# When twenty tiles are picked for routing, and where two weight pieces are decoded: one core's program for attention and experts

## The chip, the cores and the metric

One Trainium2 chip, one core of it. The metric is device time in microseconds (us) of one execution. Before the change the median of three runs is 911.4 us (911.33 to 913.87).

## The reference

Three stages follow each other. Attention with a decaying state gives 3072 rows of 384 numbers (4 batches of 768 steps, 8 heads of 48). A router then gives each row to one of 8 experts, 384 rows each, greedily by the largest score over all pairs of a row and an expert. Each expert is a two-layer network with a rectifier. Last comes a gated network that all rows share.

```python
for t in range(S):
    cur = np.einsum('bhd,bhe->bhde', u[None] * kt, vt)
    y[:, :, t] = np.einsum('bhd,bhde->bhe', rt, state + cur)
    state = w[None, :, :, None] * state + np.einsum('bhd,bhe->bhde', kt, vt)
...
flat = (x @ w_gate).flatten()
for idx in np.argsort(-flat):
    tok, e = (int(idx) // E, int(idx) % E)
    if assigned[tok] >= 0 or counts[e] >= cap:
        continue
    assigned[tok] = e
    counts[e] += 1
...
out[mask] = np.maximum(x[mask] @ w1[e], 0.0) @ w2[e]
...
return (a * b @ w_out)      # a = x @ w_a, b = x @ w_b
```

## The kernel before, in words

The program is written for five in-order engines and no scheduler reorders it: what stands earlier in the Python text of an engine's work is issued earlier on that engine.

**Attention** is a loop over 24 tiles of 128 rows, j = 0 to 23 (L715). An iteration works on several tiles at once. SP issues the loads of tile j+3 (`load_na`, `load_rk`) and j+2 (`load_va`). POOL makes q and K of tile j+3 (`prep_a`, L558, L559, L599). DVE makes `kh` and `rh` of tile j+2 (L611, L615) and sums q of that tile (`cc`, L607); ACT spreads `cc` on diagonals (L620). PE makes the scores of tile j+1 into the one buffer `pair` (L627), and DVE copies them under a mask (L631): since `pair` is single, the scores of the next tile wait for this copy. Then PE makes the rows and router scores of tile j-1 (`rows`, L676), DVE sums those into `LG` (L680), and PE makes the output of tile j (`y_out`, L662 and L666). From j = 20 on the state is no longer updated.

**Decoding.** The weights of the last network come as 64-bit numbers. A piece of 128x384 is fetched by SP (L85) and decoded by one ACT pass (L92), four DVE instructions (L95, L97, L99, L101), and a copy on ACT with a subtraction on POOL (L103, L104). 24 pieces belong to `w_a` and `w_b`, 12 to `w_out`. `EARLY` (L41) is how many of the 24 are decoded in attention, one an iteration: piece k is fetched at j = k, its ACT pass stands in j = k+1, the rest in j = k+2 (`side`, L716). In attention the DVE instructions work in a PSUM bank, later in SBUF. The other pieces and `w_out` are decoded by the generator `late` (L999). It is advanced once after every few matmuls of the expert stage (`step`, L901); a piece takes as many steps as its inner loop has rounds.

**Routing.** The greedy assignment is found by eight searches. The first needs `pick` (L159: ten small DVE instructions that find each row's best expert and its key) and `compare` (L199: the keys against 128 limits, four tiles to an instruction unit), for all 24 tiles; `head` (L214) does both for a range of tiles. Twenty tiles are done inside the loop, four after it, and PE counts the flags (`count`, L209). What `pick` and `compare` read (`un`, `steps`, and more) is set by POOL in iteration 20 (L756 to L769). The later searches (`route`, `settle`) run on DVE beside the experts' matmuls, as generators advanced by the same `step`.

**Experts.** For each of eight experts: weights gathered by POOL, split in two parts by ACT and POOL (L804, L805), matmuls L893 and L933, with ACT, DVE and POOL between them (L937, L938, L966, L969, L971, L972).

Of the kernel before, what the change touches and what calls it, by code (L numbers as in the profile page):

```python
# [37 lines left out]
DELAY = 0.8  # L38
LATE = 0, 1, 3, 5, 7
PACE = 0.8, 0.9, 0.8, 1.2  # L40
FIRST, EARLY = 2, 21  # L41
LEAST, MOST = (float(np.int32(x).view(np.float32)) for x in (0x38000000, 0x47EFFFFF))


def tile_kernel(tc, rkt, nat, wt, ub, wg, ca, cf, w12, wa, wb, wo, out):
    nc = tc.nc
    v, act, pool, pe = nc.vector, nc.scalar, nc.gpsimd, nc.tensor
    with ExitStack() as ctx:
# [23 lines left out]
        def small():  # L72
            return shared[:, 0:128]
# [9 lines left out]
        def fetch64(src, space, bufs):  # L83
            raw = space.tile([128, 768], I32, name="raw64", bufs=bufs)
            nc.sync.dma_start(raw, src.bitcast(I32))  # L85
            return raw

        def decode64(dst, raw, space, bufs):
# [18 lines left out]
        wab_pieces = [(WAB[i][:, d, q], (wa, wb)[i][d * 128:(d + 1) * 128, q * 384:(q + 1) * 384])  # L107
                      for q in range(4) for i in range(2) for d in range(3)]
# [50 lines left out]
        def pick(ml, s, kd):  # L159
            m, ki, top, q, i = [x[:, s] for x in best[:5]]  # L160
            ohu = best[5][:, :, s].rearrange("p e t -> p t e")
            n = s.stop - s.start
            b = m.bitcast(I32)

            def e(a):
                return a[:, :, None].to_broadcast([128, n, NE])

            rv = revb[:, None, :].to_broadcast([128, n, NE])
            v.tensor_reduce(m, ml[:, s], axis=AX, op=OP.max)
            yield 0.5  # L170
            v.tensor_tensor(q, ml[:, s], e(m), op=OP.is_equal)
            v.tensor_scalar(ki, b, 31, 0x7fffffff, op0=OP.arith_shift_right, op1=OP.bitwise_and)
            yield 0.5
            v.tensor_tensor(q, q, rv, op=OP.mult)
            v.tensor_tensor(ki, b, ki, op=OP.bitwise_xor)
            v.tensor_reduce(i, q, axis=AX, op=OP.max)
            yield 0.5
            if kd is not None:
                v.tensor_scalar(top, ki, 25, None, op0=OP.arith_shift_right)
            v.tensor_tensor(q, rv, e(i), op=OP.is_equal)  # L180
            if kd is not None:
                v.tensor_scalar(kd[:, s], top, 64.0, None, op0=OP.add)
            v.tensor_tensor(ohu, q, e(un[:, s]), op=OP.mult)  # L183
            yield 0.5
# [11 lines left out]
        def flags(T):  # L196
            return [wide([384 // T, T, 4]) for _ in range(T // 64)]

        def compare(ge, T, kd, s):  # L199
            n = 1536 // T  # L200
            while s.start < s.stop:
                g, end = s.start // n, min(s.stop, s.start // n * n + n)
                a, b = (s.start - g * n) // 4, (end - g * n) // 4
                v.tensor_tensor(ge[g][:, a:b], steps[:, None, 0:T].to_broadcast([128, b - a, T, 4]),
                                kd[:, s.start:end].rearrange("p (a c) -> p a c", c=4)[:, :, None]
                                .to_broadcast([128, b - a, T, 4]), op=OP.is_le)
                s = slice(end, s.stop)
# [6 lines left out]
        def head(parts):  # L214
            T = ROUNDS[0][0]
            if parts[0].start == 0:
                K["ge"] = flags(T)
                K["kd"] = R.tile([128, NT], BF, name="kd", bufs=2)
                K["cnt"] = small()[0:T, 0:NE]
            s = slice(parts[0].start, parts[-1].stop)  # L220
            for _ in pick(LG, s, K["kd"]):
                pass
            for x in parts:
                compare(K["ge"], T, K["kd"], x)
# [280 lines left out]
        with ExitStack() as actx:  # L505
# [95 lines left out]
            def prep_a(j):  # L601
                prep_q(j)
                prep_k(j)

            def prep_cc(j):
                CC[j] = A.tile([128, NH], F32, name="cc", bufs=2)
                v.tensor_reduce(CC[j], Q[j], axis=AX, op=OP.add)  # L607
# [14 lines left out]
            def scores(j):  # L622
                ps = pair.rearrange("p (g a t) -> p g a t", g=2, a=4)
                for i in range(4):
                    for g in range(2):
                        o = slice(g * 64, g * 64 + HD)
                        pe.matmul(ps[:, g, i], KH[j][o, i], RH[j][o, i], start=True, stop=True)  # L627
                return ps

            def masked(j, ps):  # L630
                v.copy_predicated(AT[j].rearrange("p g a t -> p (g a) t"), mask[:, None, :].to_broadcast([128, 8, 128]),  # L631
                                  ps.rearrange("p g a t -> p (g a) t"))
# [82 lines left out]
            for j in range(NT):  # L715
                def side(n):  # L716
                    if 0 <= j + n - FIRST < EARLY:
                        next(decode[j + n - FIRST])

                for n, load in ((3, load_na), (3, load_rk), (2, load_va)):  # L720
                    if j + n < NT:
                        load(j + n)
                if 0 <= j + 2 - FIRST < EARLY:
                    raws.append(fetch64(wab_pieces[j + 2 - FIRST][1], A, 3))
                if j + 3 < NT:
                    prep_a(j + 3)
                if 0 <= j + 1 - FIRST < EARLY:
                    decode.append(decode64(wab_pieces[j + 1 - FIRST][0], raws[j + 1 - FIRST], A, 3))
                side(1)
                for make in (prep_kh, prep_rh):  # L730
                    if j + 2 < NT:
                        make(j + 2)
                    side(0)
                if j == 0:
                    masked(1, scores(1))
                if j + 2 < NT:
                    prep_cc(j + 2)
                side(0)
                side(0)
                if 1 <= j < NT - 1:  # L740
                    masked(j + 1, scores(j + 1))
                    rows(j - 1)
                y_out(j)
                state(j)
                if j == NT - 1:
                    rows(j - 1)
                if j + 2 < NT:
                    prep_c(j + 2)
                state_out(j)
                side(0)  # L750
                if j == 2:
                    v.tensor_copy(rw[:, 0:8], cfs[:, 0:8])
                    v.tensor_copy(rw[:, 8:16], cfs[:, 136:144])
                    v.tensor_copy(unrev, rev)
                    v.tensor_copy(cbs, cbf)
                if j == 20:  # L756
                    for x, value in [(un, 1.0), (Aoh, 0.0), (cB, float(CAP)), (cE, float(CAP))]:
                        pool.memset(x, value)
                    pool.memset(runs, 1.0)
                    pool.memset(runs.rearrange("p (e t) -> p e t", e=NE)[:, :, 0], 0.0)  # L760
                    for k in range(NK):
                        pool.memset(groups[:, k], 128 * k)
                    for x, t in scaled.items():
                        pool.memset(t, x)
                    for k in range(4):
                        pool.memset(field.rearrange("p (h k) -> p h k", h=2)[:, :, k], 32.0 ** k)
                        pool.memset(fmask[:, k:k + 1], 31 << 5 * k)
                    pool.tensor_copy(steps, cfs[:, 8:136, None].to_broadcast([128, 128, 4]))
                    pool.tensor_copy(iota4, cbf[:, 128:256, None].to_broadcast([128, 128, 4]))  # L769
                if j == 22:  # L770
                    head([slice(0, 8), slice(8, 16), slice(16, 20)])
            rows(NT - 1)
            count(K["cnt"], K["ge"], ROUNDS[0][0], slice(0, 20))
            warm(IDLE[2], accum)
# [223 lines left out]

        def late():  # L999
            todo = [(WO[:, f], wo[f * 128:(f + 1) * 128]) for f in range(NFF)]  # L1000
            todo[9:9] = wab_pieces[EARLY:]
            raw = [fetch64(x[1], M, 2) for x in todo[:2]]
            parts = [decode64(x[0], raw.pop(0), M, 2) for x in todo[:1]]
            next(parts[0])
            for i in range(len(todo)):
                if i + 2 < len(todo):
                    raw.append(fetch64(todo[i + 2][1], M, 2))
                for n in range(9):
                    yield
                    if n == 4 and i + 1 < len(todo):  # L1010
                        parts.append(decode64(todo[i + 1][0], raw.pop(0), M, 2))
                        next(parts[1])
                    elif n in LATE:
                        next(parts[0])
                parts.pop(0)
# [95 lines left out]
```

## Time and profile before

| | |
|---|---|
| median of the runs | 911.4 us |
| the profiled execution's own time | 919.04 us |
| its span | 917.3 us |
| busy, share of the span: PE, DVE, POOL, ACT | 92%, 68%, 50%, 37% |
| attention, to the last rows of tile 23 | 0 to 146.6 us of the span |
| first search, without experts beside it | 146.6 to 180 us |
| first expert, with the second search beside it | 180 to 290 us |

The profiled execution is 7.6 us longer than the median. Times of the trace are counted from the start of its span. A row of the timeline has start, duration, engine, line, operation, output and inputs; what stands in square brackets is the idle time of that engine just before, and what ended it. Instructions of an engine overlap by some tenths of a microsecond, so the distance between two starts is a better price than a duration.

### The profile page before, as it was taken

Reading aid. Unit: us, or ns where it says so; the run is one execution under the profiler, and the core shown is the slowest. Engines: PE = TensorE matmul, PEld = TensorE weight load, DVE = VectorE, ACT = ScalarE, POOL = GpSimd, SP = SyncE. Lnnn points to the kernel's source line nnn. Section 1 sums busy time; section 2 is a strip of 40 time slices with the busy share of each in tenths; the row PEclk is TensorE's granted clock in tenths of the full one; section 3 lists DMA queues with packets and bytes.
Section 4 is the critical chain, followed back from the end, with each engine's and each line's share of the span. In section 5 each row is a group of like instructions: output and inputs, shape, how many; then the busy total and the mean of one; then the engine's idle time right before and its main releaser. Section 6 shows DMA issues by size and latency. Waiting matters only on the chain.

```text
span 917.3 us, 16061 instructions
## 1 busy us (share of the span) xinstructions
PE 845.0 (92%) x6109; PEld 811.0 (88%) x6109; DVE 627.1 (68%) x1694; ACT 341.1 (37%) x804; POOL 456.5 (50%) x509
## 2 busy tenths in 40 slices
PE   6788789789987999999999999999999899999994
PEld 6777778778977998999899989998999899999994
DVE  6899988598899878878777687778777612112111
ACT  4798972233233322332323233223322233323221
POOL 7688861442456515644463555265525654614221
PEclk7899989888998999999999999999999999999998
DMA  8889961421240203202020302030203212200000
GB/s 284 295 300 322 322 237 63 137 79 52 79 138 18 78 1 95 69 28 69 27 79 18 87 10 95 1 96 23 73 1 96 62 59 69 70 1 27 1 1 26
DMA packets 28142, 82.24 MB, mean 90 GB/s; under 512 B 4128, under 2 KB 10912, under 8 KB 28064
## 3 DMA queue, kind: packets, MB, share of 16 engines
q1 hardware_dynamic: 19872, 46.59, 14.9%
q0 software_dynamic: 8192, 34.61, 12.2%
q8 instruction: 48, 0.79, 0.3%
q14 instruction: 30, 0.25, 0.1%
HBM read 71.75 MB, written 9.44 MB: 89 GB/s over the span
## 4 chain that ended last, share of the span: by engine, by line
PE 69%; DVE 21%; DMA 3%; issue 3%; ACT 2%; SPq 1%; another core or an unknown queue 0%; POOL 0%; POOLq 0%; ACTq 0%; DVEq 0%
PE ab L893 26%; PE acc L893 24%; PE ab L933 10%; DMA rk<-in_rkt_dram 3%; DVE at L631 2%; PE pair L627 1%; PE acc L148 1%; PE acc L676 1%; PE acc L666 1%; DVE cB L491 1%; DVE sg L969 1%; DVE xt L826 1%; DVE ohu L183 1%; PE acc L662 1%; DVE mk L488 1%
## 5 line engine op out<-in xcount | busy, mean ns | idle before, releaser
L972 POOL TENSOR_TENSOR hg<-sg,hg 128x384 fp32r<-128x384 f32 x95 | 99.1, 1044 | 267.6 <-ACT hg L971 262.1
L893 PE MATMUL ab<-ym,Wb 128*128 128x384 f32 x864 | 173.5, 341 | 6.2 <-DVE sg L969 6.1
L893 PE MATMUL acc<-WO,hg 128*128 128x384 f32 x864 | 175.0, 344 | 0.0
L893 PE MATMUL ab<-ym,Wa 128*128 128x384 f32 x864 | 173.6, 342 | 0.0
L893 PEld LDWEIGHTS ab<-ym,Wb 128*128 128x128 f32 x864 | 150.6, 189 | 10.5 <-DVE sg L969 10.2
L893 PEld LDWEIGHTS acc<-WO,hg 128*128 128x128 f32 x864 | 153.9, 191 | 3.9 <-ACT sg L966 3.3
L893 PEld LDWEIGHTS ab<-ym,Wa 128*128 128x128 f32 x864 | 152.2, 191 | 1.8 <-issue 0.5
L805 POOL TENSOR_TENSOR wr<-raw,wr 128x384 fp32r<-128x384 f32 x120 | 121.3, 1035 | 55.9 <-ACT wr L804 55.5
L969 DVE TENSOR_TENSOR sg<-ab,sg 128x384 f32<-128x384 f32 (+1 forms) x98 | 53.4, 546 | 118.4 <-PE ab L893 105.4
L971 ACT ACTIVATE hg<-sg 128x384 fp32r<-128x384 f32 (+1 forms) x98 | 50.8, 520 | 198.7 <-DVE sg L969 194.1
L933 PE MATMUL ab<-xt,wr 128*128 128x384 f32 x567 | 114.0, 345 | 0.0
L893 PE MATMUL acc<-hg,wr 128*128 128x384 f32 x576 | 110.1, 338 | 0.9 <-DVE hg L938 0.9
L933 PEld LDWEIGHTS ab<-xt,wr 128*128 128x128 f32 x567 | 102.4, 195 | 0.0
L893 PEld LDWEIGHTS acc<-hg,wr 128*128 128x128 f32 x576 | 100.8, 189 | 1.3 <-DVE hg L938 1.2
L797 POOL DMA_INDIRECT raw<-in_w_dram,widx x64 | 64.3, 1005 | 54.0 <-issue 22.5
L966 ACT ACTIVATE sg<-ab 128x384 f32<-128x384 f32 x96 | 46.8, 488 | 106.9 <-PE ab L893 102.9
L804 ACT ACTIVATE wr<-raw 128x384 fp32r<-128x384 f32 x128 | 59.8, 515 | 48.4 <-PE acc L893 22.7
L938 DVE SCALAR_TENSOR_TENSOR hg<-ab,hg 128x384 fp32r<-128x384 f32 x64 | 35.5, 555 | 53.7 <-ACT hg L937 53.6
L937 ACT ACTIVATE hg<-ab 128x384 fp32r<-128x384 f32 x64 | 31.5, 492 | 87.0 <-PE ab L933 79.6
L620 ACT ACTIVATE at<-ident,cc 128x128 f32<-128x128 f32 x192 | 58.6, 394 | 3.2 <-DVE cc L607 3.2
L627 PE MATMUL pair<-rh,kh 48*128 48x128 f32 x384 | 31.4, 309 | 27.4 <-DVE at L631 24.8
L627 PEld LDWEIGHTS pair<-rh,kh 48*128 48x128 f32 x384 | 26.5, 210 | 30.6 <-DVE at L631 27.6
(213 smaller groups left out, 1211.7 us busy)
## 6 DMA issues: line engine op xcount, KB each, us to landing
rk<-in_rkt_dram SPq DMA_DIRECT2D x24, 512.0 KB, 5.5
na<-in_nat_dram SPq DMA_DIRECT2D x24, 384.0 KB, 4.7
va<-in_nat_dram SPq DMA_DIRECT2D x24, 200.0 KB, 5.6
raw<-in_wa_dram SPq DMA_DIRECT2D x12, 384.0 KB, 6.0
xrows<-xr SPq DMA_DIRECT2D x24, 192.0 KB, 3.4
raw<-in_wb_dram SPq DMA_DIRECT2D x12, 384.0 KB, 5.8
raw<-in_wo_dram SPq DMA_DIRECT2D x12, 384.0 KB, 3.0
raw<-in_w_dram,widx POOLq DMA_INDIRECT x64
```

The lines of the kernel that those rows point to most:

```text
L620: act.activation(AT[j][:, h % 2, h // 2], ident, AF.Copy, scale=CC[j][:, h:h + 1])
L627: pe.matmul(ps[:, g, i], KH[j][o, i], RH[j][o, i], start=True, stop=True)
L797: pool.indirect_dma_start(out=RAW[p, f], out_offset=None, in_=w12f, in_offset=bass.IndirectOffsetOnAxis(ap=WIDX[p][:, f:f + 1], axis=0))
L804: act.activation(t[:, 0], raw, AF.Copy)
L805: eng.tensor_tensor(t[:, 1], raw, t[:, 0].bitcast(F32), op=OP.subtract)
L893: pe.matmul(dst, lhs(a), rhs(b), start=first and i == 0, stop=last and i == 2)
L933: pe.matmul(ph, WR[p, f, 0][:, a, d * 128:(d + 1) * 128], XT[p][:, b, d], start=i == 0, stop=i == 8)
L938: v.scalar_tensor_tensor(t[:, 1], ph, 0.0, t[:, 0].bitcast(F32), op0=OP.max, op1=OP.subtract)
L966: act.activation(sg, pab[0], AF.Copy)
L969: v.tensor_tensor(sg[:, c], pab[1][:, c], sg[:, c], op=OP.mult)
L971: act.activation(t[:, 0, c], sg[:, c], AF.Copy)
L972: (v if end else pool).tensor_tensor(t[:, 1, c], sg[:, c], t[:, 0, c].bitcast(F32), op=OP.subtract)
```

## The change

Twenty tiles are picked in two steps: tiles 0 to 15 at the end of iteration 20, tiles 16 to 19 at the end of iteration 22, where all twenty were before. POOL's setting of what these need moves from iteration 20 to iterations 14, 15, 16 and 18. `EARLY` falls from 21 to 19: pieces 19 and 20 are no longer fetched and decoded in iterations 19 to 22 but by `late`, which now has 17 pieces instead of 15, takes 8 steps for each instead of 9, and begins the five pieces of `w_a` and `w_b` after seven of `w_out` instead of nine.

```diff
-FIRST, EARLY = 2, 21
+FIRST, EARLY = 2, 19
...
-                if j == 20:
+                if j == 14:
                     for x, value in [(un, 1.0), (Aoh, 0.0), (cB, float(CAP)), (cE, float(CAP))]:
                         pool.memset(x, value)
                     pool.memset(runs, 1.0)
                     pool.memset(runs.rearrange("p (e t) -> p e t", e=NE)[:, :, 0], 0.0)
+                if j == 15:
                     for k in range(NK):
                         pool.memset(groups[:, k], 128 * k)
...
+                if j == 16:
                     pool.tensor_copy(steps, cfs[:, 8:136, None].to_broadcast([128, 128, 4]))
+                if j == 18:
                     pool.tensor_copy(iota4, cbf[:, 128:256, None].to_broadcast([128, 128, 4]))
+                if j == 20:
+                    head([slice(0, 8), slice(8, 16)])
                 if j == 22:
-                    head([slice(0, 8), slice(8, 16), slice(16, 20)])
+                    head([slice(16, 20)])
...
-            todo[9:9] = wab_pieces[EARLY:]
+            todo[7:7] = wab_pieces[EARLY:]
...
-                for n in range(9):
+                for n in range(8):
```

**DVE from the router scores of tile 19 to the masked copy of tile 22** (L680 `LG`; L611, L615, L607 prepare tile 23; L95 to L101 decode piece 19; L631 is the masked copy). Before:

```order
L680 TENSOR_REDUCE LG<-acc_69 128x8
L611 TENSOR_TENSOR kh<-rk,table_106 128x512
L95 TENSOR_SCALAR acc_70<-mag 128x384
L615 TENSOR_TENSOR rh<-rk,table_105 128x512
L97 TENSOR_SCALAR acc_70<-acc_70 128x384
L607 TENSOR_REDUCE cc<-q 128x8
L99 SCALAR_TENSOR_TENSOR acc_70<-raw_1767,acc_70 128x384
L101 SCALAR_TENSOR_TENSOR mag<-raw_1767,acc_70 128x384
L631 COPY_PREDICATED at<-mask,pair 128x1024
```

Now, from the second half of the pick of tiles 0 to 15 on:

```order
L176 TENSOR_REDUCE i<-q 128x16
L179 TENSOR_SCALAR top<-ki 128x16
L180 TENSOR_TENSOR q<-cbs,i 128x128
L182 TENSOR_SCALAR kd<-top 128x16
L183 TENSOR_TENSOR ohu<-q,un 128x16x8
L204 TENSOR_TENSOR wide<-steps,kd 128x1024
L204 TENSOR_TENSOR wide<-steps,kd 128x512 x2
L611 TENSOR_TENSOR kh<-rk,table_106 128x512
L615 TENSOR_TENSOR rh<-rk,table_105 128x512
L607 TENSOR_REDUCE cc<-q 128x8
L631 COPY_PREDICATED at<-mask,pair 128x1024
```

The four decode instructions are gone, and ten instructions of the pick and three of the compare (L169 to L204) stand ahead of `kh`.

**POOL at the same place** (q and K of tile 23, then the subtraction of a decoded piece). Before:

```order
L559 TENSOR_TENSOR q<-q,na 128x384
L599 TENSOR_TENSOR KT_144<-na,kn 128x384
L104 TENSOR_TENSOR Wa<-mag,Wa 128x384
L758 MEMSET un 128x24
L758 MEMSET Aoh 128x192
```

Now:

```order
L559 TENSOR_TENSOR q<-q,na 128x384
L599 TENSOR_TENSOR KT_144<-na,kn 128x384
L104 TENSOR_TENSOR Wa<-mag,Wa 128x384
L802 DMA raw<-in_w_dram,widx 128x768 x2
L817 DMA row<-xrows,idx 128x384 x3
```

The three tensor instructions stay; what followed them in the loop has moved up to iterations 14 to 18 or left attention.

**DVE in the second search, in the first expert** (L204 are the compares for which PE waits; L95 to L101 are the decoding by `late`). Before:

```order
L183 TENSOR_TENSOR ohu<-q,un 128x24x8
L204 TENSOR_TENSOR wide<-steps,kd 128x512 x2
L938 SCALAR_TENSOR_TENSOR hg<-ab_2438,hg 128x384
L95 TENSOR_SCALAR mag<-mag 128x384
L204 TENSOR_TENSOR wide<-steps,kd 128x512
L97 TENSOR_SCALAR mag<-mag 128x384
L204 TENSOR_TENSOR wide<-steps,kd 128x512
L99 SCALAR_TENSOR_TENSOR mag<-raw_2711,mag 128x384
L204 TENSOR_TENSOR wide<-steps,kd 128x512 x2
```

Now:

```order
L183 TENSOR_TENSOR ohu<-q,un 128x24x8
L95 TENSOR_SCALAR mag<-mag 128x384
L97 TENSOR_SCALAR mag<-mag 128x384
L204 TENSOR_TENSOR wide<-steps,kd 128x512 x2
L943 SCALAR_TENSOR_TENSOR hg<-ab_2428,hg 128x384
L99 SCALAR_TENSOR_TENSOR mag<-raw_2698,mag 128x384
L204 TENSOR_TENSOR wide<-steps,kd 128x512 x2
L101 SCALAR_TENSOR_TENSOR mag<-raw_2698,mag 128x384
L204 TENSOR_TENSOR wide<-steps,kd 128x512 x2
```

The decode instructions come sooner: two stand ahead of the first compares where none did, and four ahead of the last where three did.

## Rows read from the trace of the kernel before

**Rows 1.** Page: the chain that ended last, shares of the span by engine.
```profile
PE 69%; DVE 21%; DMA 3%; issue 3%; ACT 2%; SPq 1%; another core or an unknown queue 0%; POOL 0%; POOLq 0%; ACTq 0%; DVEq 0%
```
**Rows 2.** Chain in order of time (start, us, what): two loads of attention.
```profile
101.97 7.79 DMA rk<-in_rkt_dram
...
127.75 5.63 DMA rk<-in_rkt_dram
```
**Rows 3.** Timeline, DVE, iterations 20 to 23 and the last pick.
```profile
132.59 0.18 DVE L680 TENSOR_REDUCE LG<-acc 128x8 f32<-128x32 f32 x1
133.40 0.69 DVE L611 TENSOR_TENSOR kh<-rk,table 128x512 f32<-128x512 f32 x1 [0.63 <-DMA rk<-in_rkt_dram]
...
137.05 1.29 DVE L631 COPY_PREDICATED at<-mask,pair 128x1024 f32<-128x1024 int32 x1
138.33 0.54 DVE L95 TENSOR_SCALAR acc<-mag 128x384 f32<-128x384 f32 x1
...
140.58 1.31 DVE L631 COPY_PREDICATED at<-mask,pair 128x1024 f32<-128x1024 int32 x1
141.87 0.31 DVE L169 TENSOR_REDUCE m<-LG 128x20 f32<-128x160 f32 x1
...
144.13 2.29 DVE L204 TENSOR_TENSOR wide<-steps,kd 128x1024 bf16<-128x1024 bf16 x4
...
146.87 0.19 DVE L169 TENSOR_REDUCE m<-LG 128x4 f32<-128x32 f32 x1
...
148.09 0.45 DVE L204 TENSOR_TENSOR wide<-steps,kd 128x512 bf16<-128x512 bf16 x1
```
**Rows 4.** Timeline, PE: scores after a long wait, and at the end of attention.
```profile
114.78 2.08 PE L627 MATMUL pair<-rh,kh 48*128 48x128 f32 x16 [2.42 <-DVE at L631]
...
121.71 0.53 PE L640 MATMUL shared<-va,KT 128*48 128x48 f32 x16
...
135.83 1.08 PE L666 MATMUL acc<-at,va 128*48 128x128 f32 x16
138.39 1.16 PE L627 MATMUL pair<-rh,kh 48*128 48x128 f32 x16 [1.48 <-DVE at L631]
...
142.48 1.16 PE L662 MATMUL acc<-rh,SD 128*128 128x128 f32 x8
```
**Rows 5.** Timeline, POOL: one subtraction in iteration 14, then iteration 20.
```profile
95.13 1.01 POOL L104 TENSOR_TENSOR Wb<-mag,Wb 128x384 fp32r<-128x384 f32 x1 [0.63 <-ACT Wb L103]
...
132.98 1.00 POOL L559 TENSOR_TENSOR q<-q,na 128x384 f32<-128x384 f32 x1
133.94 1.01 POOL L599 TENSOR_TENSOR KT<-na,kn 128x384 f32<-128x384 f32 x1
135.19 1.01 POOL L104 TENSOR_TENSOR Wa<-mag,Wa 128x384 fp32r<-128x384 f32 x1 [0.24 <-ACT Wa L103]
```
**Rows 6.** Line L180 of the pick: ns min/median/max of nine, and one beside POOL.
```profile
L180 DVE TENSOR_TENSOR q<-cbs,i x9: 193/353/897, 143.2 to 710.7; 128x192 bf16<-128x192 bf16 x7, 128x160 bf16<-128x160 bf16 x1, 128x32 bf16<-128x32 bf16 x1
...
710.39 1.02 POOL L972 TENSOR_TENSOR hg<-sg,hg 128x384 fp32r<-128x384 f32 x1 [3.72 <-ACT hg L971]
...
710.73 0.89 DVE L180 TENSOR_TENSOR q<-cbs,i 128x192 bf16<-128x192 bf16 x1
```
**Rows 7.** PE's longest wait, 180 to 291 us: us in total, times, longest.
```profile
PE shared L212 <- DVE wide L204: 4.9, 5, 2.4
```
**Rows 8.** Stretches: busy PE, PEld, DVE, ACT, POOL; clock, DMA share, GB/s.
```profile
185.00:209.00 24.00, 18.23 (x116) 17.00 (x116) 23.62 (x54) 8.37 (x19) 11.34 (x11) 0.86 0.19 61
...
265.00:290.00 25.00, 19.87 (x106) 18.74 (x105) 24.41 (x64) 7.35 (x18) 13.48 (x13) 0.93 0.13 44
```
**Rows 9.** DVE groups by line, 185 to 290 us: busy us, mean ns.
```profile
L99 DVE SCALAR_TENSOR_TENSOR mag<-raw,mag 128x384 int32<-128x384 int32 x14 | 11.4, 811 | 0.2
L101 DVE SCALAR_TENSOR_TENSOR mag<-raw,mag 128x384 int32<-128x384 int32 x14 | 8.4, 602 | 0.2
L95 DVE TENSOR_SCALAR mag<-mag 128x384 f32<-128x384 f32 x14 | 7.2, 516 | 0.0
L97 DVE TENSOR_SCALAR mag<-mag 128x384 int32<-128x384 int32 x14 | 6.8, 486 | 0.3
```

## The prediction

> **What bounds the kernel now.** I read first the chain that ended last: PE holds 69% of the span and DVE 21% [rows 1], so a microsecond of PE is a microsecond of time, and DVE counts where PE waits for it. The change touches two such places. The one is the end of attention, read in the timelines of DVE, PE and POOL from iteration 20 on; the reader is to see there which DVE instruction lets PE begin its last unbroken run. The other is the first expert, read in the list of PE's waits and in busy time by stretch: PE waited 4.9 us for the compares of the second search [rows 7], in a stretch in which DVE was busy for 23.62 of 24 us [rows 8].
>
> At the end of attention DVE finished the scores of tile 19 at 132.77, stood 0.63 us for the load of tile 23, and began `kh` at 133.40; the masked copy of tile 22 began at 137.05 [rows 3]. PE had stood for 1.48 us and went on at 138.39 with the scores of tile 23 [rows 4]. From there PE did the scores, one set of rows, both outputs and the last rows with no gap: attention ends as late as that masked copy ends plus a fixed run of PE. The pick of twenty tiles lay beside this run: it began at 141.87, and its compares took 2.29 us from 144.13 on [rows 3], beside PE's second output, which began at 142.48 [rows 4]. It cost little where it stood. So the price of the new order is: when does the masked copy of tile 22 begin?
>
> **The change, part by part, at the end of attention.** The path from `kh` to that copy was 137.05 - 133.40 = 3.65 us and held three preparations and four decode instructions. The same four alone, one iteration later, took 140.58 - 138.33 = 2.25 us [rows 3]. So without piece 19 the path is 1.4 us by difference; three times the 0.69 of `kh` would be 2.1. I take 1.6, nearer to the difference, as starts overlap.
>
> Ahead of it now stand the pick and the compare of sixteen tiles. A pick took 144.13 - 141.87 = 2.26 us for twenty tiles and 148.09 - 146.87 = 1.22 for four, so 2.0 for sixteen; the compare took 2.29 for twenty and 0.45 for four, so 1.8 [rows 3]. Together 3.8 us. If nothing disturbs them they run from 132.77 to 136.6, the load lands inside that, and the masked copy begins at 136.6 + 1.6 = 138.2, against 137.05: **1.1 us late**. That is the lower end.
>
> But they will be disturbed. POOL makes q and K of tile 23 and a subtraction just then: 132.98 to 133.98, 133.94 to 134.95, 135.19 to 136.20 [rows 5]. An instruction of the pick that met a POOL multiply of 1.02 us took 0.89 us, ending where the multiply ended plus its usual length; its median is 0.353 [rows 6]. Attention's other DVE work passed POOL undisturbed, so this meeting is new here. If one locked instruction is held by each of the three, the last gets through at 136.2, and about 0.5 us of pick and 1.8 of compare remain: 138.5, and the copy begins at 140.1, **3.0 us late**. I take this one, since POOL is busy for three of the 3.4 us that the pick needs to start clear. The rows show the holding for this one instruction plainly; where the others of its kind may pass, the value falls towards 1.1.
>
> The Trainium skill (SBUF — State Buffer, "Who interferes with whom") goes further than these rows: a VectorE instruction with two SBUF inputs, and one in a two-port mode, blocks against a GpSimd instruction that reads SBUF, while a reduction never does. By it the second, third and fourth instruction of the pick would each meet a POOL instruction, 1.4 us of pick would be left at 136.2, and the copy would be 4.0 us late instead of 3.0. No row of this case shows the second or fourth one held.
>
> **PE's clock.** Before the scores of tile 23 PE would stand 1.48 + 3.0 = 4.5 us. After a wait of 2.42 us the same scores took 2.08 us instead of 1.16, and the four groups from the scores to the output took 121.71 - 114.78 = 6.93 us against 142.48 - 138.39 = 4.09 after the wait of 1.48 [rows 4]: the matmuls ran at the lower level, half of the full clock, and **2.8 us** were lost. I take that loss in full, since PE's run from there to the end of attention has no gap to absorb it. If the wait stays at 1.1 + 1.48 = 2.6 us it is still above 2.42, but so close that it may go either way; there I take nothing, and the loss is in the range.
>
> What leaves costs nothing more and gains nothing more: ACT's and POOL's passes for the two pieces and two fetches of 384 KB on SP's queue were beside PE's waits for DVE; the 0.63 us for the load is covered by the pick. SP's later stores of rows only move up. POOL's settings in iterations 14 to 18 are a few tenths each; POOL stood 0.63 us in such an iteration before its subtraction [rows 5], and q and K are made an iteration ahead of their use, so a delay is caught up. If that cover were gone, what an iteration's settings take beyond 0.63 us would be added to it, in four iterations at most. The second pick of four tiles (1.22 + 0.45 us) falls in DVE's wait for the last rows.
>
> **In the first expert.** Two pieces more are decoded there. On DVE one costs 0.516 + 0.486 + 0.811 + 0.602 = 2.4 us as a mean with the holding by POOL in it [rows 9], two cost 4.8: the upper end. The lower end is 0, if all of it falls where PE runs on. It does not: with 8 steps instead of 9 the instructions come sooner, and by the order printed for the second search one more of them stands ahead of the last compare that PE waits for. By the same order one more stands in the next chain from the search's result to the one-hot tables, and two more in the stretch from 265 to 290 us, where DVE was busy for 24.41 of 25 us and PE for 19.87 [rows 8]. Four instructions at 0.5, the price of the two short ones, which come sooner most often, make **2.0 us**. The other four find gaps where PE is full. ACT (8.37 of 24 us) and POOL (11.34 of 24) have room for the two passes each adds, and the DMA share of 0.19 leaves room for the fetches [rows 8]. The pieces are not late: the first of them is used at step 117 by the loops, and all five are done by step 96 where three were by step 108.
>
> **Sum.** 3.0 + 2.8 + 2.0 = 7.8 us slower. Against the profiled execution's 919.04 that is 926.8; that execution is 7.6 us above the median of the runs shown, and the metric is the median, so 911.4 + 7.8 = 919.2. The bounds: 1.1 + 0 + 0 = +1.1, and 4.0 + 2.8 + 4.8 = +11.6.
>
> **The rivals.** *POOL holds, the clock stays.* The masked copy is 3 us late but the matmuls keep full clock, as after the wait of 1.48 us. 3.0 + 2.0 = +5.0: 916.4. Against it: the wait would be three times that one.
>
> *POOL does not matter.* The pick slips between POOL's instructions, +1.1, and one microsecond of decoding shows: +2.1, or 913.5, which a measurement cannot tell from no change. For it: three starts of POOL leave small gaps, and only one instruction of the pick is seen held in my rows.
>
> *The load of the last tile is late, and the pick fills a hole: faster.* The place is `kh` of tile 23. In the trace its load took 5.63 us in the chain and cost 0.63 us of DVE, but another one held the chain for 7.79 us [rows 2], and the plain runs are 7.6 us shorter than the profiled one, so their waits need not lie where the trace has them. If in them the load lands after the end of the pick, from about 137 to 138.5, 3.5 to 5 us later than traced, the pick is free, the path from the load is 1.6 instead of 3.65, and with two fetches of 384 KB gone from beside it the load itself may come sooner, by an estimated 1 us of its 5.63. PE's wait would have been 5 us before and a drop of the clock with it, which may go: -2.05 - 1 - 2.8 + 2.0 = -3.9, so 907.5. Against it: by this point the loads are nearly over, and DVE waited only once.
>
> **How the numbers follow.** About 0.3% or 2.7 us is what a measurement of this kernel can tell from no change: 908.7 to 914.1. The forecast has 0.42, the full clock with POOL's holding 0.20, the undisturbed pick 0.18, the late load 0.17; 0.03 is for a search delayed by the whole 4.8 us. That gives faster 0.18, same 0.17, slower 0.65. The likeliest is 919.2. The range goes from 908.5, which takes in half of the late-load case, to 922.5, near the sum of the upper ends; less than 2 in 10 is left out.
>
> **What would show it.** Right: in the changed profile the first pick has L172, L180 or L183 longer than alone, beside POOL's L559, L599 or L104; the masked copy of tile 22 begins 3 us later counted from the scores of tile 19; PE stands over 4 us before the scores of tile 23, and these take some 2.1 us; PE's waits in the first expert grow by 2 us. Wrong: those scores begin no later than before, or take 1.16 us; `kh` of tile 23 waits for its load after the pick; PE's waits for DVE in the first expert are no longer than now.

## The result, and the profile after

After the change the kernel takes 921.34 us (median of 12 runs, 917.65 to 926.4), before it 912.11 us (12 runs of the same comparison). These two medians lie 9.2 us apart. The ratio of the comparison, which I use throughout, is 1.0081, with a 95% interval from 1.0063 to 1.01: slower by 7.4 us, between 5.7 and 9.1. The forecast was 7.8 us more, 919.2 us, in a range from 908.5 to 922.5.

The profiled execution after took 920.48 us with a span of 918.7, only 1.4 us more than that of before. The two aren't comparable as a whole: in the profile of before, loads earlier in attention were late and the router scores of tile 19 came at 132.59 us, in that of after at 126.33, and the run with two pieces decoded twice (below), whose attention is that of before, had them at 126.65. So I compare by stretches: (1) from the router scores of tile 19 to the start of the last rows (L676 for tile 23, a group of 16 matmuls), and (2) from there to the end of the span.

The page of after, the chain that ended last, shares by engine, against [rows 1]:

```profile
PE 66%; DVE 27%; issue 3%; DMA 1%; ACT 1%; POOL 1%; SPq 0%; POOLq 0%; DVEq 0%; ACTq 0%
```

DVE stands in the chain with 27% where it had 21%. The timeline of DVE of after, from the scores of tile 19 to the masked copy of tile 23, against [rows 3] (start, duration, and in brackets the wait before):

```profile
126.33 0.17 DVE L680 TENSOR_REDUCE LG<-acc 128x8 f32<-128x32 f32 x1
126.42 0.26 DVE L169 TENSOR_REDUCE m<-LG 128x16 f32<-128x128 f32 x1
126.72 0.95 DVE L171 TENSOR_TENSOR q<-LG,m 128x128 bf16<-128x128 f32 x1
127.59 0.97 DVE L172 TENSOR_SCALAR ki<-m 128x16 int32<-128x16 int32 x1
...
128.93 0.17 DVE L179 TENSOR_SCALAR top<-ki 128x16 int32<-128x16 int32 x1
129.04 1.07 DVE L180 TENSOR_TENSOR q<-cbs,i 128x128 bf16<-128x128 bf16 x1
...
130.50 1.57 DVE L204 TENSOR_TENSOR wide<-steps,kd 128x1024 bf16<-128x1024 bf16 x3
131.98 0.68 DVE L611 TENSOR_TENSOR kh<-rk,table 128x512 f32<-128x512 f32 x1
...
133.64 1.28 DVE L631 COPY_PREDICATED at<-mask,pair 128x1024 f32<-128x1024 int32 x1
...
137.16 1.29 DVE L631 COPY_PREDICATED at<-mask,pair 128x1024 f32<-128x1024 int32 x1 [2.18 <-PE pair L627]
```

POOL of after at the same time, against [rows 5]:

```profile
126.52 1.00 POOL L559 TENSOR_TENSOR q<-q,na 128x384 f32<-128x384 f32 x1
127.48 1.06 POOL L599 TENSOR_TENSOR KT<-na,kn 128x384 f32<-128x384 f32 x1
128.97 1.00 POOL L104 TENSOR_TENSOR Wa<-mag,Wa 128x384 fp32r<-128x384 f32 x1 [0.43 <-ACT Wa L103]
```

Three instructions of the pick are long, and each ends where one of POOL's three has ended: L171 at 127.67 behind L559 (127.52), L172 at 128.56 behind L599 (128.54), L180 at 130.11 behind L104 (129.97). The copy of tile 22 begins 133.64 - 126.33 = 7.31 us after the scores of tile 19; before it was 137.05 - 132.59 = 4.46 [rows 3]. It is 2.85 us late.

PE of after, from the end of the output of tile 21 to the last rows, against [rows 4]:

```profile
129.56 1.08 PE L666 MATMUL acc<-at,va 128*48 128x128 f32 x16
134.97 2.08 PE L627 MATMUL pair<-rh,kh 48*128 48x128 f32 x16 [4.33 <-DVE at L631]
136.97 2.03 PE L676 MATMUL acc<-iw,yt 128*128 128x104 f32 x8
138.80 1.44 PE L662 MATMUL acc<-rh,SD 128*128 128x128 f32 x8
140.18 1.08 PE L666 MATMUL acc<-at,va 128*48 128x128 f32 x16
...
143.28 2.03 PE L676 MATMUL acc<-iw,yt 128*128 128x104 f32 x16
```

PE stands for 4.33 us where it stood for 1.48, and its next 16 matmuls take 2.08 us instead of 1.16; the granted clock was 0.50 of full speed from 135 to 139 us. Stretch 1 takes 143.28 - 126.33 = 16.95 us, against 11.99 before (the last rows began there at 144.58): **+4.96**.

The three longest of PE's waits of after, 180 to 291 us, against [rows 7] (us in total, times, longest):

```profile
PE ab L898 <- DVE sg L974: 4.3, 2, 2.2
PE shared L212 <- DVE wide L204: 4.0, 3, 2.5
PE ab L480 <- DVE sums L476: 3.6, 1, 3.6
```

And the two stretches of [rows 8] in after (busy PE, PEld, DVE, ACT, POOL; clock, DMA share, GB/s); the experts begin 1.3 us earlier here, so the work in them is not quite the same:

```profile
185.00:209.00 24.00, 18.48 (x102) 17.36 (x102) 23.38 (x61) 7.75 (x17) 8.50 (x8) 0.76 0.17 50
265.00:290.00 25.00, 17.80 (x93) 16.33 (x92) 24.45 (x66) 8.68 (x20) 12.03 (x12) 0.93 0.13 40
```

Stretch 2 takes 918.7 - 143.28 = 775.42 us, against 917.3 - 144.58 = 772.72: **+2.70**. The compares, in which I saw the cost, account for less than before (4.0 against 4.9); the time went elsewhere in the first experts, where DVE is as full as it was.

### The profile page after: what moved, and what is told of

Its sections match the earlier page's. It is cut to its first block, busy times and chain, and to the rows that moved or that the text cites. A ratio compares the mean times of both kernels' runs of the same rounds, so it can differ in the third digit from the quotient of the medians.

```text
span 918.7 us, 16075 instructions
## 1 busy us (share of the span) xinstructions
PE 845.7 (92%) x6109; PEld 811.0 (88%) x6109; DVE 631.6 (69%) x1704; ACT 340.9 (37%) x804; POOL 454.6 (49%) x509
## 4 chain that ended last, share of the span: by engine, by line
PE 66%; DVE 27%; issue 3%; DMA 1%; ACT 1%; POOL 1%; SPq 0%; POOLq 0%; DVEq 0%; ACTq 0%
PE ab L898 26%; PE acc L898 24%; PE ab L938 10%; DVE at L631 3%; DVE kh L611 1%; DVE mk L488 1%; DVE mag L99 1%; PE pair L627 1%; DVE sg L974 1%; DVE acc L97 1%; DVE cB L491 1%; DVE xt L831 1%; DVE cc L607 1%; DVE ohu L183 1%; DVE acc L99 1%
## 5 line engine op out<-in xcount | busy, mean ns | idle before, releaser
L898 PE MATMUL ab<-ym,Wb 128*128 128x384 f32 x864 | 175.6, 344 | 6.4 <-DVE sg L974 6.3
L620 ACT ACTIVATE at<-ident,cc 128x128 f32<-128x128 f32 x192 | 58.5, 390 | 6.0 <-DVE cc L607 6.0
```

The lines of the kernel that those rows point to most:

```text
L620: act.activation(AT[j][:, h % 2, h // 2], ident, AF.Copy, scale=CC[j][:, h:h + 1])
L898: pe.matmul(dst, lhs(a), rhs(b), start=first and i == 0, stop=last and i == 2)
```

## The experiments

All eleven runs in one table: ratio to the kernel before with its 95% interval, and from each one's profile, in us, the masked copy of tile 22 after the scores of tile 19, PE's wait ahead of the scores of tile 23, the time that these take, and the two stretches.

| run | ratio | copy of 22 | wait | scores | stretch 1 | stretch 2 |
|---|---|---|---|---|---|---|
| before | 1 | 4.46 | 1.48 | 1.16 | 11.99 | 772.72 |
| before, second profile | 1 | 5.58 | 2.60 | 1.16 | 13.11 | 771.03 |
| after | 1.0081 (1.0063 to 1.01) | 7.31 | 4.33 | 2.08 | 16.95 | 775.42 |
| picks alone | 1.0083 (1.0066 to 1.01) | 9.29 | 6.31 | 2.08 | 19.42 | 772.64 |
| decoding alone | 1.0007 (0.9989 to 1.0025) | 2.20 | 0 | 1.16 | 10.90 | 773.92 |
| two pieces decoded twice | 1.0049 (1.0034 to 1.0064) | 3.73 | 0.76 | 1.16 | 11.26 | 775.89 |
| matmuls as filler | 1.005 (1.0027 to 1.0073) | 6.45 | 0 | 1.16 | 14.43 | 776.86 |
| pick in iteration 21 | 1.0002 (0.9981 to 1.0023) | 2.19 | 0 | 1.16 | 10.90 | 773.91 |
| and nine steps | 1.0065 (1.0044 to 1.0087) | 2.20 | 0 | 1.16 | 10.91 | 776.06, 779.49 |
| one piece moved | 1.0001 (0.9982 to 1.002) | 2.37 | 0 | 1.16 | 10.92 | 770.82 |
| POOL waits | 1.0076 (1.0049 to 1.0103) | 5.29 | 2.32 | 1.75 | 16.00 | 772.84 |
| POOL waits, filler | 1.0036 (1.001 to 1.0062) | 5.29 | 0 | 1.16 | 12.85 | 773.57 |

**The picks alone.** After's picks and POOL's settings, with before's decoding:

```diff
-FIRST, EARLY = 2, 19
+FIRST, EARLY = 2, 21
...
-            todo[7:7] = wab_pieces[EARLY:]
+            todo[9:9] = wab_pieces[EARLY:]
...
-                for n in range(8):
+                for n in range(9):
```

> Only the picks in two steps, with POOL's settings moved; all pieces decoded where they were. Theory A (the loss is mostly the pick ahead of the masked copy of tile 22): the pick still costs its 2.9 us there, and the four decode instructions stand in the path again, 2.05 us, so the copy is 5 us late counted from the scores of tile 19, PE's clock falls after a wait of over 6 us and costs 2.1 us, the expert stage is as before: about 7 us over the kernel before, 919. Theory B (the loss is mostly the two pieces in the experts): at most 2 us over before, 914.

1.0083, or +7.6 us. Stretch 2 is before's within 0.1 us, stretch 1 is 7.43 longer: here the four decode instructions of piece 19 come between the pick and the copy as well, so PE stands 6.31 us. The picks alone cost as much as the whole change, all of it in attention.

**The decoding alone.** After, with one pick of twenty tiles in iteration 22 as before:

```diff
-                if j == 20:
-                    head([slice(0, 8), slice(8, 16)])
                 if j == 22:
-                    head([slice(16, 20)])
+                    head([slice(0, 8), slice(8, 16), slice(16, 20)])
```

> Only the two pieces moved to the experts; one pick of twenty tiles at the end of iteration 22 as before. Theory A: the masked copy of tile 22 comes 2.05 us sooner than before, PE's clock stays, the expert stage takes some 2.7 us more: +0.7 us, 912.8. Theory B: the whole 7 to 9 us, 919 to 921.

1.0007: no change that can be measured. The copy of tile 22 comes 2.26 us sooner than before, but stretch 1 gains only 1.09, for DVE then stands 3.79 us ahead of the copy of tile 23 until ACT has spread that tile's `cc` on diagonals (L620). Stretch 2 gives 1.2 us back.

**Two pieces decoded twice.** Before, with pieces 19 and 20 decoded by `late` a second time at after's pace:

```diff
-            todo[9:9] = wab_pieces[EARLY:]
+            todo[7:7] = wab_pieces[19:]
...
-                for n in range(9):
+                for n in range(8):
```

> The kernel before, with pieces 19 and 20 decoded a second time among the experts by the new pacing (17 pieces, 8 steps each); the output is the same. Theory A: attention unchanged, expert stage 2.7 us longer: 914.8. Theory B: 7 to 9 us longer, 919 to 921.

1.0049, or +4.5 us (3.1 to 5.9 by the interval), where 2.7 were expected; the profile, of the fastest of the seven executions (915.58 us, median 919.45), has 3.2 in stretch 2 and 0.7 less in stretch 1, in which no load was late this time. The decoding in the experts does cost, then. By the ratios the run with the decoding alone, which decodes the same there, is 3.8 us shorter than this one. Stretch 1 shows only 0.4 of that (10.90 against 11.26); where the rest comes from is not shown.

**Matmuls as filler.** After, with matmuls without use on PE ahead of the scores of tile 23, into a bank that is free there:

```diff
+                if j == 22:
+                    warm(70, lambda: accs[2])
```

> The changed kernel with 70 matmuls of ones into an unused bank ahead of the scores of tile 23, which fill about 3.9 us of PE's wait. If the fall of the clock is a term of its own: the scores take 1.16 instead of 2.08 us, and 2.1 us come back, 919.2. If only the late copy counts: no change, 921.3.

1.005 against 1.0081, with intervals that overlap. The scores take 1.16 us: with PE kept busy over the wait its clock stays full, though the copy of tile 22 is 2.0 us late here too. Stretch 1 is 2.52 us shorter than in after, but 0.86 of that is an earlier copy. In this execution L171 began at 131.31 us, just ahead of POOL's L599 at 131.32, and took 0.29 us; L180 took 0.29 too, L172 took 0.97, and the compares beside L104 took 2.13 (1.57 in after). So what POOL holds differs between executions. The other 1.66 us are the clock's. The 70 matmuls reached past the copy: it ended at 138.65 and the scores began at 139.16, where in after only 0.05 us lie between. Without that half microsecond the clock's part is again 2.1 us.

**The first pick one iteration later.**

```diff
-                if j == 20:
+                if j == 21:
                     head([slice(0, 8), slice(8, 16)])
```

> The kernel after, with one thing changed: the pick of tiles 0 to 15 stands at the end of iteration 21 instead of iteration 20, so behind the masked copy of tile 22, where DVE of the run with the decoding alone stood for 3.79 us before the masked copy of tile 23, and where POOL has nothing left to do in the loop. Theory A (the pick's place costs attention, by its length on the path, by POOL's holding and by PE's half clock after the long wait): the locked instructions L172 and L180 take their undisturbed 0.17 to 0.3 us; the masked copy of tile 22 begins 2.2 us after the router scores of tile 19 (7.31 in the kernel after), the scores of tile 23 take 1.16 us, and attention from those router scores to the last rows takes about 10.9 us instead of 16.95. The expert stage keeps its +1.2 to +2.7 us. Ratio to before 1.000 to 1.003, some 6 us below the kernel after. Theory B (any pick ahead of the last masked copies delays them): the masked copy of tile 23 comes late by what of the pick does not fit the hole, up to 1 us or more, and the last rows with it; ratio 1.003 to 1.006.

Theory A, to the tenth: stretch 1 took 10.90 us, and 1.0002 is no change from before. Of DVE in this run:

```profile
133.48 1.32 DVE L631 COPY_PREDICATED at<-mask,pair 128x1024 f32<-128x1024 int32 x1 [0.32 <-ACT at L620]
...
135.09 0.29 DVE L171 TENSOR_TENSOR q<-LG,m 128x128 bf16<-128x128 f32 x1
135.30 0.17 DVE L172 TENSOR_SCALAR ki<-m 128x16 int32<-128x16 int32 x1
...
136.00 0.29 DVE L180 TENSOR_TENSOR q<-cbs,i 128x128 bf16<-128x128 bf16 x1
...
138.67 1.30 DVE L631 COPY_PREDICATED at<-mask,pair 128x1024 f32<-128x1024 int32 x1 [0.42 <-ACT at L620]
```

The same pick of sixteen tiles costs nothing behind the copy of tile 22: it fills DVE's wait for ACT, of which 0.42 us is left, and with POOL done L171, L172 and L180 take 0.29, 0.17 and 0.29 us. So the loss is the place of the pick, not its work.

**Nine steps for the first seven pieces**, on top of the last run:

```diff
-                for n in range(8):
+                for n in range(9 if i < 7 else 8):
```

> The run with the first pick in iteration 21, and in addition the first seven pieces that the generator decodes beside the experts (all of w_out) take 9 steps each, as before the change, the later ten 8 steps. Theory A (the cost in the expert stage is DVE work that stands sooner ahead of the second search's compares): with the old pace beside the second search PE's longest group of waits for those compares is as before, and the time from the last rows to the end of the span falls by about 1 us against that run; ratio to before 0.998 to 1.002. Theory B (the cost is the two pieces themselves, wherever they stand): no difference from that run beyond 0.2%.

A miss, to the other side: before's pace made it slower, 1.0065 against 1.0002. Busy PE in the profile of the pick in iteration 21, 30 to 122 and 122 to 160 us after the start of the last rows:

```profile
172.19:264.19 92.00, 82.81 (x542) 78.37 (x540) 83.37 (x197) 33.25 (x73) 43.80 (x42) 0.90 0.35 105
264.19:302.19 38.00, 29.97 (x160) 27.73 (x160) 36.42 (x104) 12.98 (x29) 23.46 (x27) 0.96 0.23 72
```

and with nine steps:

```profile
169.14:261.14 92.00, 80.93 (x552) 76.11 (x551) 81.14 (x197) 32.53 (x71) 41.46 (x40) 0.95 0.33 101
261.14:299.14 38.00, 28.65 (x139) 27.08 (x139) 36.66 (x96) 12.30 (x28) 22.81 (x24) 0.87 0.22 62
```

PE stands 11.07 + 9.35 = 20.4 us instead of 9.19 + 8.03 = 17.2, with DVE busy 36.66 of 38 us. Since the runs lost more (4.9 us) than this profile (2.1), I took it a second time:

> The run with nine steps for the first seven pieces, unchanged, for a second profile, since its first showed a loss of 2.1 us in the experts where the runs showed 4.9 us. Theory A (the loss is in the experts in every execution): from the last rows to the end 776 us again, the same loss between the transposes of the second and the matmuls of the third expert's weights. Theory B (it is chance): within 1 us of the 773.9 us of the run with eight steps.

779.49 us in stretch 2, worse still, with 20.2 us of PE's standing in these 130 us. It isn't chance; but the size varies by 3.4 us between two executions, and nine steps aren't the milder order. Which of the shifted instructions does it was not tried.

**One piece moved instead of two**: before, with `EARLY` at 20, so that eight pieces of `w_out` come first (with 9 steps, the others with 8), and with the decode instructions of the last piece behind the copy of tile 22:

```diff
...
+                if j == 21:
+                    for _ in range(4):
+                        side(0)
...
```

> The kernel before, with 20 pieces decoded in attention instead of 21 (so one more by the generator, before which eight pieces of w_out stand, the first eight with 9 steps, the others with 8), all twenty tiles picked once in iteration 22, and in iteration 21 the four decode instructions of the last piece behind the masked copy of tile 22 instead of ahead of it. Theory A: attention gains what the run with the decoding alone gained, about 1.1 us from the router scores of tile 19 to the last rows, and the expert stage loses half of what two pieces lost, 0.6 to 1.3 us: ratio 0.999 to 1.001. Theory B (the four instructions behind the copy of tile 22 delay that of tile 23, for which DVE has a hole of 3.79 us, enough for their 2.2 us): no gain in attention, ratio 1.001 to 1.003.

1.0001, as theory A has it: stretch 1 gains 1.07 us, and DVE still waits 1.38 us for ACT ahead of the copy of tile 23. Stretch 2, 770.82 us, shows nothing of the 0.6 to 1.3 us that theory A adds in the experts; executions vary by more than that. No version here beats the kernel before by a difference that can be measured.

**POOL waits for the pick.** The pick of after stays in iteration 20 (where `head` now comes just ahead of the last `side`), but POOL does `L559`, `L599` and `L104` behind its compare:

```diff
...
+                    head([slice(0, 8), slice(8, 16)])
+                    pool.tensor_copy(steps[:, 0:8], cfs[:, 8:16, None].to_broadcast([128, 8, 4]))
+                    pool.tensor_mul(q23, q23, NA[23][:, D:2 * D])
+                    prep_k(23)
                 side(0)
...
```

> The kernel after with the pick of tiles 0 to 15 left in iteration 20, but POOL kept away from it: its second multiply for q and its multiply for K of tile 23 (L559, L599), and the subtraction of a decoded piece (L104), come behind the end of the compare (POOL first sets eight columns of the limits, which the compare reads, to the values they have). The first multiply for q (L558) stays ahead. Theory A (POOL holds the pick): L171, L172 and L180 take 0.29, 0.17 and 0.29 us instead of 0.95, 0.97 and 1.07, so the masked copy of tile 22 begins 2.1 us sooner, 5.2 us after the router scores of tile 19 instead of 7.31, where it was 4.46 before the change; PE's wait before the scores of tile 23 is 2.2 us instead of 4.33. If that is short enough for the full clock the scores take 1.16 us and attention from tile 19's scores to the last rows 12.8 us, ratio to before 1.003 to 1.004; if not, 2.08 us and 14.9 us, ratio 1.005 to 1.006. Theory B (the pick's own length at this place is the cost): the copy begins 7 us after, no difference to the kernel after, ratio 1.008.

DVE of this run:

```profile
130.66 0.18 DVE L680 TENSOR_REDUCE LG<-acc 128x8 f32<-128x32 f32 x1
...
131.06 0.29 DVE L171 TENSOR_TENSOR q<-LG,m 128x128 bf16<-128x128 f32 x1
131.27 0.17 DVE L172 TENSOR_SCALAR ki<-m 128x16 int32<-128x16 int32 x1
...
131.97 0.29 DVE L180 TENSOR_TENSOR q<-cbs,i 128x128 bf16<-128x128 bf16 x1
...
135.95 1.29 DVE L631 COPY_PREDICATED at<-mask,pair 128x1024 f32<-128x1024 int32 x1
```

and its PE:

```profile
137.29 1.75 PE L627 MATMUL pair<-rh,kh 48*128 48x128 f32 x16 [2.32 <-DVE at L631]
138.97 2.03 PE L676 MATMUL acc<-iw,yt 128*128 128x104 f32 x8
140.80 1.95 PE L662 MATMUL acc<-rh,SD 128*128 128x128 f32 x8
142.68 1.95 PE L666 MATMUL acc<-at,va 128*48 128x128 f32 x16
```

The holding is gone: the copy of tile 22 comes 2.02 us sooner, 5.29 us after the scores of tile 19, so POOL's holding is 2.0 us. (It is 2.17 at `kh`, 5.65 against 3.48 us after those scores; in this run `cc` then waits 0.15 us for POOL's late q.) The 0.83 us that remain are a balance: the 3.4 us of the pick and its compares, less the decode instructions that left and the wait for the load that it covers. Yet the whole is 1.0076. After a wait of 2.32 us the clock still fell, to 0.50 of full speed from 138 to 144 us, and for longer than in after: stretch 1 without the copy's own delay is 16.00 - 5.29 = 10.71 us, where before had 11.99 - 4.46 = 7.53 and after 16.95 - 7.31 = 9.64.

**The same, with 38 matmuls as filler**, ahead of the scores of tile 23 as above:

> The run in which POOL waits for the pick, and in addition 38 small matmuls without use (some 2.2 us) on PE in iteration 22, ahead of the scores of tile 23, into a bank that is free there. Theory A (three separate terms: the length of the pick, POOL's holding, PE's half clock): with the holding and the half clock both gone, the scores of tile 23 take 1.16 us, and attention from tile 19's scores to the last rows takes 12.8 us, 0.8 more than in the profile before the change where it was 11.99; with some 2.7 us of the experts the ratio to before is 1.003 to 1.005. Theory B (the half clock comes by the length of the iteration, not by PE's standing still): scores of 1.75 us or more again, attention 15 to 16 us, ratio 1.007.

PE of this run:

```profile
130.62 2.29 PE L148 MATMUL acc<-ones 128*128 128x128 bf16 x38
133.04 1.16 PE L627 MATMUL pair<-rh,kh 48*128 48x128 f32 x16
```

Stretch 1 took 12.85 us, forecast 12.8, and the ratio is 1.0036. The copy comes as in the last run, only PE was kept busy (granted clock 1.00 throughout): 3.15 us of stretch 1 were the half clock. By the runs it is 1.0076 against 1.0036, with intervals that overlap a little.

**The kernel before, a second profile:**

> The kernel before, unchanged, for a second profile. Theory A (its first profile was 7.6 us above the median because of late loads and clock falls ahead of tile 19): the router scores of tile 19 come some 5 us sooner than 132.59 us, and from the last rows of tile 23 to the end of the span it takes 772.7 us again, within 1 us. Theory B (the variation from run to run lies beside the experts): tile 19 at the same time, and another time from the last rows to the end.

The signs of theory B came: tile 19's scores at 132.66 us again, and stretch 2 took 1.7 us less. But that does not explain why this execution too, with 918.55 us, lies 5.7 us above the median of its comparison, for its stretch 2 is the shorter one. In it the load of tile 23 was late by more than in the first. Its DVE, and its PE:

```profile
134.59 0.69 DVE L611 TENSOR_TENSOR kh<-rk,table 128x512 f32<-128x512 f32 x1 [1.75 <-DMA rk<-in_rkt_dram]
```

```profile
104.26 2.08 PE L627 MATMUL pair<-rh,kh 48*128 48x128 f32 x16 [2.21 <-DVE at L631]
...
139.58 1.16 PE L627 MATMUL pair<-rh,kh 48*128 48x128 f32 x16 [2.60 <-DVE at L631]
```

A wait of 2.21 us was followed by half clock here, one of 2.60 us was not.

## Why the prediction was right

**The masked copy of tile 22: 3.0 us late forecast, 2.85 measured.** Its parts hold too. The pick and the compare without POOL took 134.14 - 130.75 = 3.4 us (forecast 3.8), the way from `kh` to the copy 133.64 - 131.98 = 1.66 us (1.6), the lateness without holding is 0.83 (1.1), the holding 2.0 (1.9). What I had wrong is which instructions are held: I gave each of POOL's three one of L172, L180 and L183; it was L171, L172 and L180, and L183 passed at 0.74 us when POOL was done. The trace of before had a second case, which I left out of my rows: an L172 of 1.00 us at 274.82, beside POOL's L972 (1.52 us from 274.27), where its median is 0.17. L171 was never held there (at most 0.43). That L171 and L172 are held as well is what the Trainium skill states (SBUF — State Buffer, "Who interferes with whom"); the trace agrees with the rule, and its reduction L169 took 0.26 us beside POOL's L559. I also read the row of L180 as ending its usual length after the multiply; there it was 0.21 us, and the three in after end 0.02 to 0.15 us behind POOL. The lateness that I worked out by the rule, 4.0 us, was too much, for L174 to L179 slipped through in POOL's gap of 0.43 us.

**The clock: 2.8 us forecast, 2.1 in the profile after, 3.2 between the two runs in which POOL waits.** That it is a term by itself is shown by the filler: with a copy as late as in the run beside it, the matmuls that keep PE busy took stretch 1 from 16.00 to 12.85 us. The rival by which POOL holds and the clock stays, 916.4 us, falls. The one by which POOL doesn't matter had the price of the pick right and would not have been spared: at a wait of 2.32 us the clock fell all the same, the case which I had left at nothing.

**The experts: 2.0 us forecast, +2.70 in the profile after.** With 17 pieces at 8 steps, stretch 2 took 774.6 us as a mean of seven executions (772.84 to 776.86); with before's decoding 772.1 as a mean of three (771.03 to 772.72): 2.5 us, by their spread good to an estimated 1.6. The size holds, the place doesn't. Stretches of the profile before, 30 to 122, 122 to 160 and 297 to 338 us after the start of the last rows:

```profile
174.58:266.58 92.00, 82.51 (x534) 77.71 (x532) 78.06 (x192) 30.87 (x67) 40.55 (x40) 0.88 0.32 98
266.58:304.58 38.00, 30.74 (x162) 29.30 (x161) 35.25 (x96) 12.40 (x28) 23.77 (x25) 0.91 0.20 62
441.58:482.58 41.00, 38.85 (x228) 37.40 (x227) 34.12 (x105) 12.84 (x28) 21.71 (x26) 1.00 0.17 53
```

and of after:

```profile
173.28:265.28 92.00, 81.50 (x531) 76.75 (x531) 82.55 (x197) 32.52 (x70) 43.00 (x42) 0.91 0.34 103
265.28:303.28 38.00, 29.91 (x149) 28.31 (x148) 34.65 (x97) 12.03 (x27) 21.94 (x23) 0.87 0.21 66
440.28:481.28 41.00, 38.85 (x219) 37.56 (x218) 33.67 (x99) 12.08 (x27) 20.72 (x23) 0.96 0.14 44
```

In the first two PE stood 16.7 us before and 18.6 after: 1.8 us, with DVE's 78.06 us of the first grown to 82.55. Over all profiles PE stood 16.5 to 16.8 us in these two stretches with before's decoding (three) and 16.8 to 19.5, 18.4 as a mean, with after's (seven): some 1.7 us more, near the 2.0 forecast. The step that failed is "one more of them stands ahead of the last compare that PE waits for": the waits for compares fell by 0.9 us (to 4.0; the second profile of before has 4.1), and 3.6 us of waiting stand at L480. But L480 can't be blamed either, for the second profile of before has a wait of 3.3 us there with no instruction moved. In the third stretch PE is as busy in both, and nine matmuls fewer got done at a clock of 0.96 than at 1.00. The second profile of before has 0.96 there as well, so this part belongs to the execution, not surely to the change. Which of the moved instructions makes PE stand longer remains open.

**The late load**, my rival that ended faster, has its ground: the load cost DVE 0.63 and 1.75 us in the two profiles of before, and nothing in the run with two pieces decoded twice, whose attention is the same. In after the pick covers it, as forecast. It is a microsecond or two against 5, and in no profile here is the pick free in iteration 20.

**The sum.** 4.96 + 2.70 = 7.7 us in the profiles, 7.4 by the runs, 7.8 forecast. That it comes so close is partly luck: the clock was taken 0.7 us too high and the experts 0.7 too low. The table gives sums for other runs too: for the picks alone 7.43 - 0.08 = 7.4 against 7.6 measured, with POOL waiting and the filler 0.86 + 2.5 (the experts' mean) = 3.4 against 3.3. For the decoding alone and the pick in iteration 21, -1.1 + 2.5 = 1.4 against 0.6 and 0.2 is inside their intervals. For the two pieces decoded twice it does not close: -0.7 + 2.5 = 1.8 against 4.5.

## What to carry to other kernels

Work put on an engine that waits later costs by the place where it stands: the same pick, 3.4 us of DVE undisturbed, cost 6 us of attention ahead of a copy for which PE waits (16.95 against 10.90 us), and nothing behind it, in a hole where DVE waits for ACT. Price such a move by what the delayed engine loses afterwards: a net delay of 0.8 us became 2.9 by the meeting with POOL and 5.0 by PE's clock. And taking away one of these alone may bring next to nothing (1.0081 to 1.0076), as long as the wait that remains still brings the clock down.

## What the runs showed of the hardware

VectorE's shift on 16 columns (L172, 0.17 us alone) took 0.97 us beside a GpSimd multiply of 1.06: what this meeting cost went by the length of the neighbour, not by the instruction's own. L171, which in the run with 70 matmuls as filler began 0.01 us ahead of the same multiply, took 0.29 us.

The length of a wait alone does not say whether TensorE's clock falls: after 2.21, 2.32 and 2.42 us [rows 4] of standing still its matmuls ran at half clock (1.2 instead of 2.4 GHz), after 2.60 us they ran at full, and after 2.37 us as well (the scores at 121.63 in the run with two pieces decoded twice, 1.16 us). Nor does it say for how long: after 4.33 us the loss was 2.1 us, after 2.32 it was 3.2, and after 6.31 (the picks alone, 10.13 against 7.53 us from the copy on) 2.6.

Executions of one kernel differ by 1.7 and 3.4 us between the last rows and the end (771.03 and 772.72 before, 776.06 and 779.49 with nine steps): a difference of 2 us in the experts can't be read from one profile of each.
